# Two places for the exponentials of the first five units of an attention and FFN kernel

## The chip, the cores and the metric

The kernel runs on one core of a Trainium2 chip. A core has a tensor engine (PE; its weight loads are listed apart, as PEld), a vector engine (DVE), a scalar engine (ACT), GpSimd (POOL) and a queue that issues DMAs (SP). PE reads SBUF and writes PSUM; ACT and DVE read and write both. Each engine works through its own queue of instructions in order and waits where an instruction needs the result, or the buffer, of another engine. The metric is the device time of one execution in microseconds (us).

## The reference

Sparse attention for 8 batches of 8 heads, 576 positions and a head size of 64, and on its output an FFN with softplus:

```python
scores = scale * np.matmul(q, k.transpose(0, 1, 3, 2))
thresh = np.max(scores, axis=-1, keepdims=True) - tau
scores = np.where(scores >= thresh, scores, -1000000000.0)
scores = scores - np.max(scores, axis=-1, keepdims=True)
attn = np.exp(scores)
attn = attn / (np.sum(attn, axis=-1, keepdims=True) + 1e-09)
attn_out = np.matmul(attn, v)
x = attn_out.transpose(0, 2, 1, 3).reshape(B * S, H * D)
h = x @ w_in
g = np.maximum(h, 0.0) + np.log1p(np.exp(-np.abs(h)))
out = g @ w_out
```

x has 4608 rows of 512 columns, and the FFN is 2048 wide. Everything is float32.

## The kernel before, in words

**Units and tiles.** Two heads of a batch make a unit; there are 32. A unit's 2 x 576 query rows are 9 tiles of 128: tiles 0 to 3 belong to the first head, 5 to 8 to the second, and tile 4 (`NC`) holds the last 64 rows of both. `mate` (L451) names pairs: (0,1), (2,3), (5,6), (7,8); tile 4 is alone. 288 tiles run one after the other.

**What a tile passes through.** `scores` (L406) multiplies queries and keys into one of two PSUM banks, which tiles take by turns. `row_max` (L427) takes the negated row maximum and the threshold on DVE (L430, L431). `exps` (L434) writes exp(score - maximum), 128 x 576, into one half of `e_all` on ACT (L435). `mask` (L438) sets to zero on DVE, in place, what lies below the threshold, and adds up the rows (L440). `weights_T` (L458) transposes the 576 columns on PE, since the value product needs them in partitions: four transposes of 128 columns (L474), and the remaining 64 columns. `weights_hi` (L493) copies the transposed values to SBUF on ACT (L498, L510 to L514), `values` (L542) multiplies them with v.

**The halves of `e_all`.** `e_all` is 128 x 2 x 576. A tile in half 0 has its 512 main columns first and its 64 remaining ones last; a tile in half 1 has them the other way round (the keys are laid out as 64, 512, 64 columns, and `scores` starts at column 64 or at column 0). So the remaining columns of both halves lie side by side, and one transpose (L471), issued with the second tile of a pair, takes the 128 columns of both. The lone tile transposes its own 64 (L477). Before the change halves alternate from tile to tile over the whole kernel; since a unit has nine tiles, a pair's first tile is in half 0 in even units and in half 1 in odd ones.

**Whole units.** The first `NF = 5` units are "whole" (`s.whole`): their weights and values stay in float32, and the value products (L549) are float32 matmuls. Later units split weights into upper and lower parts (`group`, L444, tags `gH` and `gL` with two buffers each), which DVE computes (L132, a helper's line), and multiply both (L555, L556). So no buffer of the tag `gL` is used before unit 5.

**The order of the work.** A loop over the tiles (L924) goes through a string of steps, for tile g: `PAT0` for the first 36 tiles (`TG`), `PAT` after that.

```python
PAT = "ThRlefmpfxSvwp"
PAT0 = "RMTeShlfpfxvwp"
```

R is the row maximum of tile g+1, M the mask of tile g (m: of tile g+1), T its transposes, e the exponentials of tile g+1, S the scores of tile g+2, h and l the upper and lower parts of tile g, v three float32 value products, f FFN matmuls, x the next unit's splits and transposes, w and p the preparation of weights and steps put off. In the first 36 tiles transposes go to PSUM banks of their own (`tm`, `tr`), after that into the bank of the tile's scores (`s`).

From these calls the framework lays out each engine's queue: a step that comes first in the source has precedence, but one that is ready earlier by the framework's own estimate can go ahead. It also adds the waits, from the tiles and columns that instructions read and write.

**The preparation of weights** shares the queues in the first 60 or so tiles: for each of 32 pieces a load (SP, L185), then L193 on ACT, L194 on POOL, L200, L202 and L205 on DVE, and a split on POOL (lines 125 and 132 of helpers). Pieces of `w_in` are written back to DRAM (L234).

**The FFN** works in chunks of 512 rows: `hidden` (L632; matmuls L645, L647, L649), softplus on ACT (L667), `project` (L694; L703, L705, L707). Its matmuls begin with tile 41, are spread over the tiles, and fill the end alone.

Of the kernel before, what the change touches and what calls it, by code (L numbers as in the profile page):

```python
# [9 lines left out]
F32 = mybir.dt.float32  # L10
F32R = mybir.dt.float32r
# [12 lines left out]
P = 128  # L24
# [35 lines left out]
def tile_kernel(ctx: ExitStack, tc: tile.TileContext, q, k, v, tau, w_in, w_out, out):  # L60
# [8 lines left out]
    nc = tc.nc  # L69
    B, H, S, D = q.shape  # L70
    NT, DM = out.shape
    DFF = w_in.shape[1]
    SM = 512
    SR = S - SM
    HS = S // 2
    NC = SM // P
# [8 lines left out]
    apool = ctx.enter_context(tc.tile_pool(name="apool", bufs=2))  # L85
# [11 lines left out]
    ident = identr.bitcast(F32)  # L97
# [177 lines left out]
    for b in range(B):  # L275
        for kind in (("one", "two") if b < NSPLIT else ("all",)):
            for hp in range(NPAIR):
                s = Unit()
# [5 lines left out]
                for g, (j, members) in enumerate(groups):  # L284
                    c = 0
# [113 lines left out]

    e_all = cpool.tile([P, 2, S], F32, name="e_all")
    banks = [ps_s.tile([P, 2, 512], F32, tag="s", name=f"s_{i}") for i in range(SB)]
    nth = [0]

    def scores(s, t):  # L406
        if t == s.tiles[0]:
            s.sums = apool.tile([P, 9], F32, tag="sums", name=f"sums_{s.i}")
            s.half, s.sp, s.m, s.grp = {}, {}, {}, {}
        sp = banks[nth[0] % SB]  # L410
        s.half[t] = half = nth[0] % 2
        nth[0] += 1
        s.sp[t] = sp
        if t == NC:
            parts = [(qm[:, n, j, :], j) for j in range(2) for n in range(2)]
        else:
            j = 0 if t < NC else 1
            c = t if t < NC else t - NC - 1
            parts = [(s.qT[j][n][:, c * P:(c + 1) * P], j) for n in range(2)]
        k0 = (1 - half) * SR  # L420
        for m, (lhs, j) in enumerate(parts):
            for hf in range(2):
                i = nc.tensor.matmul(sp[:, hf, 0:HS], lhs, s.kT[j][:, k0 + hf * HS:k0 + (hf + 1) * HS],  # L423
                                     start=(m == 0), stop=(m == len(parts) - 1))
        scored.append(i)
# [6 lines left out]
        s.m[t] = (negm, thr)  # L432

    def exps(s, t):  # L434
        nc.scalar.activation(e_all[:, s.half[t], :].rearrange("p (h n) -> p h n", h=2), s.sp[t][:, :, 0:HS],  # L435
                             AF.Exp, bias=s.m[t][0], scale=1.0)

    def mask(s, t):  # L438
        e2 = e_all[:, s.half[t], :].rearrange("p (h n) -> p h n", h=2)
        masked.append(nc.vector.scalar_tensor_tensor(  # L440
            out=e2, in0=s.sp[t][:, :, 0:HS], scalar=s.m.pop(t)[1], in1=e2, op0=ALU.is_ge, op1=ALU.mult,
            accum_out=s.sums[:, s.tiles.index(t):s.tiles.index(t) + 1]))
# [8 lines left out]
    def mate(s, t):  # L451

        if t == NC:
            return None, False
        u = t if t < NC else t - 1
        return (t + 1, False) if u % 2 == 0 else (t - 1, True)

    def weights_T(s, t):  # L458
        half = s.half[t]
        e = e_all[:, half, :]  # L460
        other, second = mate(s, t)
        lone = other is None
        if 9 * NPAIR * s.b + 9 * s.hp + t < TG:
            main = ps_g.tile([P, NC, P], F32, tag="g", name=f"tm_{s.i}_{t}")
            rest = ps_g.tile([P, NC, P], F32, tag="g", name=f"tr_{s.i}_{t}")[:, 0, :] if lone or second else None
        else:
            sp = s.sp[t]
            main = sp[:, 0, :].rearrange("p (c n) -> p c n", n=P)
            rest = sp[:, 1, 0:P]
        if second:  # L470
            nc.tensor.transpose(rest, e_all.rearrange("p h n -> p (h n)")[:, SM:SM + P], ident)  # L471
        for c in range(NC):
            c0 = half * SR + c * P
            nc.tensor.matmul(main[:, c, :], e[:, c0:c0 + P], ident, is_transpose=True, start=True, stop=True)  # L474
        if lone:
            r0 = 0 if half else SM
            nc.tensor.transpose(rest[0:SR, :], e[:, r0:r0 + SR], ident)  # L477
        s.sp[t] = (main, rest)
# [358 lines left out]
    for kind, g in WL:  # L837
        for m in range(4):
            n = len(prep)
# [71 lines left out]
    for n in (0, 2, 1):  # L911
        qkT(u0, 1, n)
        point()
    u0.eng, u0.eng_lo = eng, nc.gpsimd
    scores(*tiles[0])
    row_max(*tiles[0])
    exps(*tiles[0])
    scores(*tiles[1])
    for j in range(2):
        split_v(u0, j)  # L920
# [3 lines left out]
    for g, (cur, t) in enumerate(tiles):  # L924
# [5 lines left out]
        for step in PAT0 + ("m" if g == TG - 1 else "") if g < TG else PAT:  # L930
            if step == "T":
                weights_T(cur, t)
            elif step == "h":
                weights_hi(cur, t)
            elif step == "l":
                weights_lo(cur, t)
            elif step == "R" and nxt:
                row_max(*nxt)
            elif step == "e" and nxt:
                exps(*nxt)  # L940
            elif step == "m" and nxt:
                mask(*nxt)
            elif step == "M":
                mask(cur, t)
            elif step == "f":
                upto += quota / PAT.count("f")
                while done < upto:
                    done += next(ffn)
            elif step == "x":
                extras(cur.i, cur.tiles.index(t))  # L950
            elif step == "S" and g + 2 < NS:
                scores(*tiles[g + 2])
            elif step == "v":
                slow_products()
            elif step == "w":
                while prep and prep[0][0] <= g:
                    _, f, a = prep.pop(0)
                    f(*a)
            elif step == "p":
                point()  # L960
# [38 lines left out]
```

## Time and profile before

| | |
|---|---|
| median of 3 runs | 1450.28 us (1449.85 to 1451.96) |
| the profiled execution | 1450.65 us, its span 1448.9 us |
| busy over the span | PE 97%, DVE 68%, ACT 59%, POOL 41% |
| mean of one exponential (L435) | 751 ns, x288 |
| mean of one mask (L440) | 815 ns, x288 |
| mean of one row maximum (L430) | 754 ns, x288 |
| mean of one transpose (L474) | 276 ns, x1008 |
| HBM traffic | 116 GB/s over the span |

PE's ends are modelled. "Idle before" (in rows of the timeline: the number in square brackets) is the time that the engine had nothing to do just before an instruction, with the instruction that ended it. In the timeline a row gives the start in us, the length in us, engine, line, operation, output and inputs, and the number of instructions merged into it. In the page's slices each digit is the busy share of a fortieth of the span (36 us) in tenths.

### The profile page before, as it was taken

The page shows a single profiled execution, that of the slowest core. Times are in us where ns is not written, and L with a number is a line of the kernel's source. Part 1 is how long each engine was busy: PE and PEld are TensorE (multiplying, and loading weights), DVE is VectorE, ACT ScalarE, POOL GpSimd, SP SyncE. Part 2 cuts the span into 40 slices and gives each one's busy share as a digit, 9 for nine tenths or more (in the row PEclk, how much of TensorE's full clock was granted, in tenths as well). Part 3 has the DMA queues.
Part 4 walks back from the last instruction along what each step waited for, and adds up shares of the span by engine and source line. Part 5 has one row for each costly group of instructions (what it writes and reads, how often), then busy time and mean ns, then how long its engine had stood idle before and what let it go on. Part 6 is the DMA issues. An engine that isn't in the chain of part 4 may idle for free.

```text
span 1448.9 us, 23497 instructions
## 1 busy us (share of the span) xinstructions
PE 1399.3 (97%) x7860; PEld 1161.6 (80%) x7860; DVE 983.1 (68%) x2211; ACT 848.1 (59%) x1615; POOL 591.0 (41%) x619
## 2 busy tenths in 40 slices
PE   6987999999999999999999999999999999999998
PEld 4654788878888888888888888888888888788886
DVE  6977688877777777777777777777777777402111
ACT  5766767767656566657665665667665765311010
POOL 3667666544333333344334333444334431324221
PEclk9999999999999999999999999999999999999999
DMA  5767765445333533444433533354344532344321
GB/s 160 220 192 231 212 187 170 138 121 154 109 102 110 137 115 110 119 134 150 123 111 96 153 106 101 116 151 120 113 119 136 148 98 74 101 130 129 119 85 44
DMA packets 131208, 189.93 MB, mean 131 GB/s; under 512 B 35312, under 2 KB 86800, under 8 KB 131088
## 3 DMA queue, kind: packets, MB, share of 16 engines
q1 hardware_dynamic: 131088, 188.43, 44.5%
q8 instruction: 63, 1.03, 0.3%
q14 instruction: 57, 0.47, 0.1%
HBM read 140.51 MB, written 27.41 MB: 116 GB/s over the span
## 4 chain that ended last, share of the span: by engine, by line
PE 78%; DVE 7%; ACT 5%; issue 3%; DMA 3%; POOL 2%; SPq 1%; POOLq 0%; ACTq 0%; DVEq 0%
PE s L423 10%; PE h L647 9%; PE h L645 9%; PE h L649 8%; PE o L707 8%; PE o L705 7%; PE s L474 7%; PE o L703 7%; PE pv L555 3%; PE pv L556 3%; PE tr L364 2%; DVE e_all L440 2%; DVE negm L430 2%; PE pv L549 1%; POOL g L132 1%
## 5 line engine op out<-in xcount | busy, mean ns | idle before, releaser
L132 POOL TENSOR_TENSOR g<-st,g 128x512 fp32r<-128x512 f32 x144 | 191.7, 1349 | 196.3 <-DVE g L129 182.5
L440 DVE SCALAR_TENSOR_TENSOR e_all<-s,thr,e_all 128x576 f32<-128x576 f32 x288 | 234.4, 815 | 53.0 <-ACT e_all L435 49.8
L430 DVE TENSOR_REDUCE negm<-s 128x1 f32<-128x576 f32 x288 | 217.1, 754 | 43.1 <-PE s L423 34.6
L435 ACT ACTIVATE e_all<-s,negm 128x576 f32<-128x576 f32 x288 | 215.9, 751 | 39.3 <-PE tr L471 20.7
L707 PE MATMUL o<-wo_o,g 128*128 128x512 f32 x576 | 232.3, 404 | 5.3 <-POOL g L132 5.3
L703 PE MATMUL o<-wo_o,g 128*128 128x512 f32 x576 | 232.0, 403 | 1.1 <-ACT st L667 0.7
L647 PE MATMUL h<-xl,wi 128*128 128x512 f32 x576 | 232.8, 404 | 0.0
L645 PE MATMUL h<-xh,wi 128*128 128x512 f32 x576 | 229.8, 399 | 0.0
L649 PE MATMUL h<-xh,wi 128*128 128x512 f32 x576 | 229.3, 398 | 0.0
L705 PE MATMUL o<-wo_o,g 128*128 128x512 f32 x576 | 228.5, 397 | 0.0
L498 ACT CAST gH<-s 128x512 fp32r<-128x512 f32 (+1 forms) x270 | 145.0, 550 | 139.1 <-PE s L474 135.6
L132 DVE TENSOR_TENSOR gL<-s,gH 128x512 fp32r<-128x512 f32 (+1 forms) x270 | 168.8, 634 | 47.8 <-ACT gH L498 25.3
L423 PE MATMUL s<-kT,qT 128*128 128x288 f32 x1024 | 192.2, 310 | 6.2 <-ACT gH L498 1.8
L423 PEld LDWEIGHTS s<-kT,qT 128*128 128x128 f32 x1024 | 148.5, 190 | 27.9 <-issue 11.3
L474 PE MATMUL s<-identr,e_all 128*128 128x128 f32 x1008 | 155.1, 276 | 4.8 <-DVE e_all L440 4.8
L129 DVE CAST g<-st 128x512 fp32r<-128x512 f32 x128 | 57.4, 485 | 149.5 <-ACT st L667 149.0
L667 ACT ACTIVATE st<-h 128x512 f32<-128x512 f32 x144 | 78.3, 596 | 115.3 <-PE h L649 114.6
L474 PEld LDWEIGHTS s<-identr,e_all 128*128 128x128 f32 x1008 | 114.7, 141 | 22.3 <-DVE e_all L440 12.6
L707 PEld LDWEIGHTS o<-wo_o,g 128*128 128x128 f32 x576 | 108.4, 188 | 29.1 <-POOL g L132 11.0
L645 PEld LDWEIGHTS h<-xh,wi 128*128 128x128 f32 x576 | 108.3, 188 | 23.5 <-issue 1.0
L703 PEld LDWEIGHTS o<-wo_o,g 128*128 128x128 f32 x576 | 108.5, 188 | 22.2 <-DVE g L129 2.0
L649 PEld LDWEIGHTS h<-xh,wi 128*128 128x128 f32 x576 | 108.4, 188 | 21.6
(107 smaller groups left out, 2366.4 us busy)
## 6 DMA issues: line engine op xcount, KB each, us to landing
wi<-wi_d SPq DMA_DIRECT2D x144, 512.0 KB
qT<-qT SPq DMA_DIRECT2D x124, 128.0 KB
R<-r_d SPq DMA_DIRECT2D x64, 144.0 KB
kn<-in_k_dram SPq DMA_DIRECT2D x32, 256.0 KB
qn<-in_q_dram SPq DMA_DIRECT2D x32, 256.0 KB
vn<-in_v_dram SPq DMA_DIRECT2D x32, 256.0 KB
wc_i<-in_moe_w_in_dram SPq DMA_DIRECT2D x16, 512.0 KB
wi_d<-wc_i SPq DMA_DIRECT2D x32, 256.0 KB
```

What stands on the lines that cost most here:

```text
L132: eng.tensor_tensor(out=out_, in0=in_, in1=hi.bitcast(F32), op=ALU.subtract)
L423: i = nc.tensor.matmul(sp[:, hf, 0:HS], lhs, s.kT[j][:, k0 + hf * HS:k0 + (hf + 1) * HS], start=(m == 0), stop=(m == len(parts) - 1))
L430: nc.vector.reduce_max(negm, s.sp[t][:, :, 0:HS], axis=AX.XY, negate=True)
L435: nc.scalar.activation(e_all[:, s.half[t], :].rearrange("p (h n) -> p h n", h=2), s.sp[t][:, :, 0:HS], AF.Exp, bias=s.m[t][0], scale=1.0)
L440: masked.append(nc.vector.scalar_tensor_tensor(out=e2, in0=s.sp[t][:, :, 0:HS], scalar=s.m.pop(t)[1], in1=e2, op0=ALU.is_ge, op1=ALU.mult, ...
L474: nc.tensor.matmul(main[:, c, :], e[:, c0:c0 + P], ident, is_transpose=True, start=True, stop=True)
L645: nc.tensor.matmul(h, wi[:, 0, cc, :], u.h[cc], start=(cc == 0), stop=False)
L647: nc.tensor.matmul(h, wi[:, 0, cc, :], u.l[cc], start=False, stop=False)
L649: nc.tensor.matmul(h, wi[:, 1, cc, :], u.h[cc], start=False, stop=(cc == NCC - 1))
L703: nc.tensor.matmul(o, gh[:, sl], wo[fc][:, 0, :], start=(i == 0), stop=False)
L705: nc.tensor.matmul(o, gh[:, sl], wo[fc][:, 1, :], start=False, stop=False)
L707: nc.tensor.matmul(o, gl[:, sl], wo[fc][:, 0, :], start=False, stop=(i == QF - 1))
```

## The change

In the whole units the exponentials of pairs go by turns to a second place, `e_more`, and to `e_all`; the lone tile counts as a pair here. `e_more` takes one of the two buffers of the tag `gL`. Which half a tile uses now follows from its place in the pair: the first and the lone tile take half 0, the second half 1, in all 32 units. The PSUM banks go on alternating as before. Units 5 to 31 use `e_all` alone, as before, with the new numbering of halves.

```diff
     e_all = cpool.tile([P, 2, S], F32, name="e_all")
+    e_more = apool.tile([P, NC, 320], F32R, tag="gL", name="e_more").bitcast(F32)
+    e_more = e_more.rearrange("p c n -> p (c n)")[:, 0:2 * S].rearrange("p (h n) -> p h n", h=2)
+    pairs = [0]
...
         sp = banks[nth[0] % SB]
-        s.half[t] = half = nth[0] % 2
+        half = s.half[t] = int(mate(s, t)[1])
+        pairs[0] += not half
+        s.e[t] = e_more if s.whole and pairs[0] % 2 else e_all
         nth[0] += 1
...
     def exps(s, t):
-        nc.scalar.activation(e_all[:, s.half[t], :].rearrange("p (h n) -> p h n", h=2), s.sp[t][:, :, 0:HS],
+        nc.scalar.activation(s.e[t][:, s.half[t], :].rearrange("p (h n) -> p h n", h=2), s.sp[t][:, :, 0:HS],
                              AF.Exp, bias=s.m[t][0], scale=1.0)
```

`mask` and both transposes of `weights_T` (L471, L474) read and write `s.e[t]` in place of `e_all` in the same way.

More of the change, by code (lines that the diff above doesn't have):

```diff
@@ L408, in scores @@
             s.sums = apool.tile([P, 9], F32, tag="sums", name=f"sums_{s.i}")
-            s.half, s.sp, s.m, s.grp = {}, {}, {}, {}
+            s.half, s.sp, s.m, s.grp, s.e = {}, {}, {}, {}, {}
         sp = banks[nth[0] % SB]
-        s.half[t] = half = nth[0] % 2
+        half = s.half[t] = int(mate(s, t)[1])
+        pairs[0] += not half
+        s.e[t] = e_more if s.whole and pairs[0] % 2 else e_all
         nth[0] += 1
@@ L434, in exps @@
     def exps(s, t):
-        nc.scalar.activation(e_all[:, s.half[t], :].rearrange("p (h n) -> p h n", h=2), s.sp[t][:, :, 0:HS],
+        nc.scalar.activation(s.e[t][:, s.half[t], :].rearrange("p (h n) -> p h n", h=2), s.sp[t][:, :, 0:HS],
                              AF.Exp, bias=s.m[t][0], scale=1.0)
     def mask(s, t):
-        e2 = e_all[:, s.half[t], :].rearrange("p (h n) -> p h n", h=2)
+        e2 = s.e[t][:, s.half[t], :].rearrange("p (h n) -> p h n", h=2)
         masked.append(nc.vector.scalar_tensor_tensor(
@@ L459, in weights_T @@
         half = s.half[t]
-        e = e_all[:, half, :]
+        e = s.e[t][:, half, :]
         other, second = mate(s, t)
@@ L470, in weights_T @@
         if second:
-            nc.tensor.transpose(rest, e_all.rearrange("p h n -> p (h n)")[:, SM:SM + P], ident)
+            nc.tensor.transpose(rest, s.e[t].rearrange("p h n -> p (h n)")[:, SM:SM + P], ident)
         for c in range(NC):
```

## The prediction

> **What bounds the kernel now.** I read the page's busy table and its slices first, then the windows of four stretches: busy time and, in brackets, instructions of PE, PE's weight loads, DVE, ACT and POOL, then PE's granted clock, the DMA share and GB/s.
>
> ```profile
> PE 1399.3 (97%) x7860; PEld 1161.6 (80%) x7860; DVE 983.1 (68%) x2211; ACT 848.1 (59%) x1615; POOL 591.0 (41%) x619
> ...
> PE   6987999999999999999999999999999999999998
> ```
>
> ```profile
> 20.00:146.00 126.00, 106.69 (x591) 71.74 (x590) 101.82 (x215) 85.16 (x195) 83.50 (x98) 0.95 0.71 204
> 52.30:69.30 17.00, 14.44 (x90) 10.34 (x91) 16.90 (x35) 12.07 (x30) 11.57 (x14) 1.00 0.66 185
> 86.80:109.60 22.80, 21.14 (x109) 13.15 (x109) 17.50 (x40) 13.71 (x30) 16.08 (x18) 0.93 0.64 171
> 200.00:1240.00 1040.00, 1027.38 (x6067) 878.88 (x6066) 794.02 (x1819) 679.29 (x1264) 411.32 (x429) 1.00 0.42 123
> ```
>
> From 200 us on, PE has 12.6 us without work in 1040, so nothing there pays that doesn't shorten PE's own work. In the first four slices there is slack: between 20 and 146 us (the attention tiles that run before the first FFN product) PE stands still for 126.0 - 106.7 = 19.3 us and DVE for 24.2. What the change frees lies there. Who waits for whom between 18 and 150 us (us in total, times, longest):
>
> ```profile
> ACT e_all L435 <- PE tr L471: 20.7, 12, 3.0
> ...
> DVE e_all L440 <- ACT e_all L435: 14.3, 17, 2.9
> ACT wa_i L193 <- DMA wc_i<-in_moe_w_in_dram: 11.0, 6, 4.1
> ...
> DVE wa_o L200 <- POOL wa_o L194: 6.1, 7, 1.3
> ```
>
> The first line is what the change is about. An exponential (L435) writes a half of `e_all`; the transpose L471 reads 64 columns of each half. So the exponential of a pair's first tile, and of the lone tile, waits until the previous pair's second tile has been masked on DVE and transposed on PE. The second line is how much DVE feels of this, at most. The other two are waits that the change leaves: the weight preparation, whose steps stand in the same queues of ACT, POOL and DVE.
>
> **Part 1: the wait that goes.** The longest wait of a mask in units 0 to 3 shows what it is worth.
>
> ```profile
> 24.46 2.41 PE L549 MATMUL pv<-gH,vn 128*64 128x256 f32 x6
> 24.56 0.76 DVE L430 TENSOR_REDUCE negm<-s 128x1 f32<-128x576 f32 x1
> ...
> 27.16 0.74 ACT L435 ACTIVATE e_all<-s,negm 128x576 f32<-128x576 f32 x1 [2.57 <-PE tr L471]
> ...
> 27.94 0.82 DVE L440 SCALAR_TENSOR_TENSOR e_all<-s,thr,e_all 128x576 f32<-128x576 f32 x1 [2.37 <-ACT e_all L435]
> ...
> 31.45 0.63 PE L474 MATMUL tm<-identr,e_all 128*128 128x128 f32 x4 [0.35 <-DVE e_all L440]
> ...
> 34.55 0.30 PE L471 MATMUL tr<-identr,e_all 128*128 128x128 f32 x1 [0.20 <-DVE thr L431]
> ```
>
> The row maximum ends at 25.32, so with a place of its own the exponential could run at about 25.4 and the mask at 26.2, 1.7 us sooner. But L471 came late because PE itself was at value products until 26.87, and in the 8 us after it PE stood still only 0.35 and 0.20 us. So 2.37 us of DVE's wait are worth 0.55 us of time. The other masks that waited for an exponential held by L471, up to unit 3's end:
>
> ```profile
> 69.36 0.82 DVE L440 SCALAR_TENSOR_TENSOR e_all<-s,thr,e_all 128x576 f32<-128x576 f32 x1 [0.16 <-ACT e_all L435]
> ...
> 92.33 0.82 DVE L440 SCALAR_TENSOR_TENSOR e_all<-s,thr,e_all 128x576 f32<-128x576 f32 x1 [0.97 <-ACT e_all L435]
> ...
> 98.60 0.82 DVE L440 SCALAR_TENSOR_TENSOR e_all<-s,thr,e_all 128x576 f32<-128x576 f32 x1 [0.43 <-ACT e_all L435]
> ...
> 103.90 0.82 DVE L440 SCALAR_TENSOR_TENSOR e_all<-s,thr,e_all 128x576 f32<-128x576 f32 x1 [0.47 <-ACT e_all L435]
> ...
> 109.66 0.33 PE L471 MATMUL tr<-identr,e_all 128*128 128x128 f32 x1 [1.41 <-DVE e_all L440]
> ...
> 127.60 0.82 DVE L440 SCALAR_TENSOR_TENSOR e_all<-s,thr,e_all 128x576 f32<-128x576 f32 x1 [0.18 <-ACT e_all L435]
> ```
>
> Only where PE idles soon after does a wait count: 0.16, 0.47 (1.41 of idle PE follows at 109.66) and 0.18. The 0.97 and 0.43 fall in a stretch, 86.8 to 109.6, in which PE's idle time of 1.7 is little more than that 1.41. Term: 0.55 + 0.16 + 0.47 + 0.18 = 1.4 us. Bounds: 0, if the weight steps wait in the mask's place, and all six waits, 4.6 us.
>
> **Part 2: the order of the queues.** The instructions are laid into the queues anew, and an exponential that is ready sooner can stand further ahead. Two places show a price.
>
> ```profile
> 18.47 0.76 DVE L430 TENSOR_REDUCE negm<-s 128x1 f32<-128x576 f32 x1 [1.43 <-PE s L423]
> ...
> 20.45 0.78 ACT L435 ACTIVATE e_all<-s,negm 128x576 f32<-128x576 f32 x1
> ...
> 22.14 0.66 PE L474 MATMUL tm<-identr,e_all 128*128 128x128 f32 x4 [2.06 <-DVE e_all L440]
> ...
> 81.07 0.43 DVE L200 TENSOR_SCALAR wa_o<-wa_o 128x512 uint32<-128x512 uint32 x1 [1.34 <-POOL wa_o L194]
> ...
> 82.14 0.81 DVE L440 SCALAR_TENSOR_TENSOR e_all<-s,thr,e_all 128x576 f32<-128x576 f32 x1
> ...
> 83.11 0.63 PE L474 MATMUL tm<-identr,e_all 128*128 128x128 f32 x4 [0.72 <-DVE e_all L440]
> ```
>
> At the start, the exponential of 20.45 could follow its row maximum at 19.2: 1.25 of the 2.06 us in which PE idles. At 82.14 the mask stands behind a weight step that waited 1.34 us for POOL; a mask that is ready earlier would be put ahead, worth PE's 0.72. Term: 2.0 us; bounds -3 and 5. Below nothing, because an order can also turn out worse (half of L200's 6.1 us of waits, with masks behind them); 5 is a quarter of PE's 19.3.
>
> **Part 3: unit 4 and the buffer.** One more long wait of a mask lies at this stretch's end:
>
> ```profile
> 146.10 0.82 DVE L440 SCALAR_TENSOR_TENSOR e_all<-s,thr,e_all 128x576 f32<-128x576 f32 x1 [2.86 <-ACT e_all L435]
> 146.16 0.47 PE L645 MATMUL h<-xh,wi 128*128 128x512 f32 x1
> ```
>
> From here the FFN products fill PE, so I count 0; bounds 0 and 2.9. The new place is one of two buffers that lie idle until unit 5, whose second group takes it over two tiles after its last reader: 0.
>
> **Part 4: the new numbering of halves.** A pair's first tile and the lone tile 4 now both take half 0. In units 5 to 31, with `e_all` alone, tile 5's exponential therefore waits for tile 4's transposes (L474, L477), which it didn't before. Mostly it comes after them anyway, behind tile 4's copies on ACT. At six of the 27 lone tiles (the first and the last are shown) it doesn't:
>
> ```profile
> 352.41 0.76 ACT L435 ACTIVATE e_all<-s,negm 128x576 f32<-128x576 f32 x1
> ...
> 353.45 0.27 PE L477 MATMUL s<-identr,e_all 128*64 128x128 f32 x1
> ...
> 1147.97 0.76 ACT L435 ACTIVATE e_all<-s,negm 128x576 f32<-128x576 f32 x1
> ...
> 1149.02 0.27 PE L477 MATMUL s<-identr,e_all 128*64 128x128 f32 x1
> ```
>
> The exponential starts 1.05 us ahead of L477 and will start after its end, at least 1.05 + 0.27 = 1.3 us later. Queued behind it on ACT are the lone tile's copies, or they go first and it comes 2 us later; behind the mask on DVE stand that tile's lower parts, and PE's transposes of tile 5 wait for the mask. What hides this is the FFN products, which can be laid before them. How well, the waits between 200 and 1300 us tell:
>
> ```profile
> DVE e_all L440 <- ACT e_all L435: 31.8, 57, 1.4
> ...
> PE s L474 <- DVE e_all L440: 3.7, 11, 0.4
> ```
>
> Of 31.8 us in which masks waited for exponentials PE felt 3.7, or 12%. Six times 1.3 to 2.0 us is 8 to 12 us; 12% of 10 is 1.2 us. Bounds: 0 and, if the cover is gone, 12.
>
> **The sum.** 1.4 + 2.0 + 0 - 1.2 = 2.2 us gained. The profiled execution took 1450.65 us (span 1448.9, 1.75 around it), 0.4 above the median of 1450.28, so it becomes 1448.4 by its own clock and 1448.1 beside the median. This case's own range goes from 5 us gained to 1 lost. A measurement of this kernel can tell about 0.2%, 2.9 us, from no change, so most of this case counts as none.
>
> **Rivals.**
>
> 1. DVE, not PE, paces the first stage. From 52.3 to 69.3 us it is busy 16.9 of 17 us. If that holds for the stage, each wait of a mask on a held exponential is worth its whole length: 4.6 us for the six waits, 1.25 at the start, 1.34 at 81 us and 0.8 at other such weight steps, 8 us; less the 1.2 of part 4, 6.8 gained: 1443.5, between 1440 and 1446. Against it: DVE itself idles 24.2 us in the stage, 11.0 of ACT's waits hang on loads and 6.1 of DVE's on POOL. Chance 0.28. The Trainium skill ("Perfetto Trace Analysis", Identifying the Most-Contended Engine) speaks for this rival: it calls matmul busy time a poor measure of PE's headroom, asks for the weight-load share instead, and takes DVE's occupancy at its word. By that rule PE's 71.74 of 126 us (57%) leave room, and DVE at 81% is the limit.
>
> 2. Slower: tile 5's exponential (part 4) reaches PE. The wait is new and certain, and two engines stand behind it; in those six places the scheduler had brought tile 5 forward, so other products must now fill the gap. With the 3.4 of parts 1 and 2 against it, it decides once over 60% of the 10 us reach PE (6.3 lost against 3.4 gained makes 2.9, the limit); from 60% to all 12 us the time is 1453 to 1459. Against it: the 12%. Chance 0.20.
>
> 3. The freed exponential waits for something else, for L193 ahead of it on ACT (11.0 us on loads), or its mask for L200 (6.1 us). The masks move and PE's idle time stays: within 1 us of 1450.3. For it: those waits are untouched. Against it: the start, where neither stands between. Chance 0.14.
>
> **How the numbers follow.** My case 0.38 (a third of it beyond 2.9 us gained), rival 1 0.28, rival 3 0.14, rival 2 0.20. Faster by over 0.2%: 0.12 + 0.28 = 0.40. Within: 0.26 + 0.14 = 0.40. Slower: 0.20. My case's range is 1445 to 1451; the whole range goes down to 1441, into rival 1, and up into rival 2, to 1454.
>
> **What would show it.** In the changed profile the waits of L435 on L471 must be gone up to the first FFN product (20.7 us to under 2) and masks must wait less than 14.3; PE's idle time between 20 us and that product must fall by 3 to 4 us and the product start as much before 146.16. L200's waits and L193's on loads should stay, near 6 and 11. At lone tiles after unit 4 no exponential of tile 5 may start before L477 has ended, and PE's waits on masks from 200 us should stay under 6. If the first FFN product comes 6 us or more earlier, rival 1 is right; if it comes earlier and the end doesn't, part 4 is mis-sized; if masks wait less and PE idles as before, rival 3.

## The result and the profile after

The changed kernel takes 1459.55 us in the median of four runs (1457.47 to 1461.08), beside 1450.07 us for the kernel before (four runs, 1449.38 to 1451.96): a ratio of 1.0063, 95% interval [1.0047, 1.0078]. It is some 9 us slower, where 2.2 us of gain were forecast. The profiled execution took 1457.47 us; it is the fastest of the four, so the profile below accounts for some 7 of the 9 us.

From the page of the changed kernel: busy time by engine, and PE's busy share in the 40 slices.

```profile
PE 1400.6 (96%) x7860; PEld 1161.2 (80%) x7860; DVE 984.0 (68%) x2211; ACT 851.9 (59%) x1615; POOL 589.1 (40%) x619
...
PE   6878999999999999999999999999999999999998
```

The work is the same, 1400.6 us of PE after 1399.3; what was added in the profiled execution is for the most part time in which PE stands still. The windows of three stretches say where. First the row of the kernel before that the prediction didn't show, then the rows of the changed kernel (columns as there: busy time and instructions of PE, its weight loads, DVE, ACT, POOL; PE's granted clock, DMA share, GB/s).

```profile
146.00:200.00 54.00, 53.05 (x286) 39.72 (x285) 37.64 (x78) 43.20 (x85) 33.54 (x39) 1.00 0.71 214
```

```profile
20.00:146.00 126.00, 105.59 (x594) 71.94 (x592) 100.33 (x214) 85.81 (x193) 77.66 (x94) 0.96 0.66 192
146.00:200.00 54.00, 50.37 (x260) 36.69 (x260) 34.38 (x73) 40.74 (x81) 35.80 (x38) 1.00 0.77 231
200.00:1240.00 1040.00, 1025.80 (x6050) 875.53 (x6049) 794.09 (x1814) 680.77 (x1263) 410.76 (x432) 1.00 0.43 123
```

PE's idle time: 20.4 us in place of 19.3 up to 146 us, 3.6 in place of 1.0 from there to 200, 14.2 in place of 12.6 up to 1240. That is 5.4 of the 6.8 us by which the two profiled executions differ. So the loss has two parts: one in the first 200 us, where the second place works, and one in the 27 later units, where only the numbering of halves differs.

The waits between 18 and 150 us of the changed kernel (us in total, times, longest), those that answer to the rows of before. First a second row of the kernel before for L200, which the prediction left out:

```profile
DVE wa_i L200 <- POOL wa_i L194: 2.7, 3, 1.4
```

```profile
ACT wa_i L193 <- DMA wc_i<-in_moe_w_in_dram: 9.2, 7, 3.4
...
ACT e_all L441 <- DVE negm L436: 8.3, 8, 2.0
...
DVE e_more L446 <- ACT e_more L441: 7.6, 7, 2.3
ACT e_more L441 <- DVE negm L436: 6.8, 8, 1.8
...
DVE wa_i L200 <- POOL wa_i L194: 5.8, 3, 2.3
...
DVE wa_o L200 <- POOL wa_o L194: 5.5, 7, 3.2
...
DVE e_all L446 <- ACT e_all L441: 3.4, 6, 1.1
```

Exponentials (now L441) no longer wait for L477, the former L471: the 20.7 us are gone. In their place they wait 15.1 us for their own row maxima (L436). Masks (L446) wait 11.0 us for exponentials, where it was 14.3. The weight step L200 waits longer for POOL than before, 11.3 us in place of 8.8 (6.1 + 2.7), and its longest waits are 2.3 and 3.2 us, where they were 1.4 and 1.3. What that does, the timeline of the changed kernel shows near 100 us:

```profile
100.41 0.74 ACT L441 ACTIVATE e_all<-s,negm 128x576 f32<-128x576 f32 x1
...
101.69 0.43 DVE L200 TENSOR_SCALAR wa_i<-wa_i 128x512 uint32<-128x512 uint32 x1 [2.31 <-POOL wa_i L194]
...
102.03 0.75 DVE L436 TENSOR_REDUCE negm<-s 128x1 f32<-128x576 f32 x1
...
102.70 1.27 DVE L202 SCALAR_TENSOR_TENSOR wa_i<-wc_i,wa_i 128x512 uint32<-128x512 uint32 x1
...
103.89 0.20 DVE L437 TENSOR_SCALAR thr<-negm,ntau 128x1 f32<-128x1 f32 x1
104.01 0.80 DVE L446 SCALAR_TENSOR_TENSOR e_all<-s,thr,e_all 128x576 f32<-128x576 f32 x1
...
104.88 0.33 PE L477 MATMUL tr<-identr,e_all 128*128 128x128 f32 x1 [3.32 <-DVE e_all L446]
```

The exponential is done at 101.15, but its mask starts at 104.01. Ahead of it in DVE's queue stands L200, which waits 2.31 us for POOL, and behind that another row maximum, a second weight step and a threshold. PE idles 3.32 us for this one mask. Two masks followed across this place show what it costs (tiles counted from 0). The one above, at 104.01, is tile 28's. Below are tile 27's and then, from the kernel before, tile 28's; tile 27's of before starts at 98.60 and stands in the prediction.

```profile
96.57 0.81 DVE L446 SCALAR_TENSOR_TENSOR e_all<-s,thr,e_all 128x576 f32<-128x576 f32 x1
```

```profile
101.89 0.80 DVE L440 SCALAR_TENSOR_TENSOR e_all<-s,thr,e_all 128x576 f32<-128x576 f32 x1
```

Tile 27's mask comes 2.03 us sooner than before, tile 28's 2.12 us later. So just ahead of this place the changed kernel led, and the one place turns a lead of 2 us into a lag of 2. Two more places at which PE waits for a mask behind L200:

```profile
78.44 1.27 POOL L132 TENSOR_TENSOR wo_o<-wa_o,wo_o 128x512 fp32r<-128x512 f32 x1
78.50 1.48 DVE L200 TENSOR_SCALAR wa_o<-wa_o 128x512 uint32<-128x512 uint32 x1 [0.59 <-POOL wa_o L194]
...
82.17 0.85 PE L480 MATMUL tm<-identr,e_more 128*128 128x128 f32 x4 [2.19 <-DVE e_more L446]
...
87.42 1.48 DVE L200 TENSOR_SCALAR wa_o<-wa_o 128x512 uint32<-128x512 uint32 x1 [0.20 <-POOL wa_o L194]
...
90.51 0.30 PE L477 MATMUL tr<-identr,e_all 128*128 128x128 f32 x1 [2.33 <-DVE e_all L446]
```

Here L200 waits for POOL only 0.59 and 0.20 us. What holds the mask is L200 itself: it takes 1.48 us, where it took 0.43 at 101.69. The last section comes back to this. Between L200 and the mask stand a row maximum, a threshold and L202 at the first place, a threshold and L202 at the second.

After the attention tiles the first FFN products wait too, for transfers and for parts of x, which none of them did before:

```profile
147.26 0.50 PE L651 MATMUL h<-xh,wi 128*128 128x512 f32 x1 [1.41 <-DMA wi<-wi_d]
...
159.99 0.50 PE L651 MATMUL h<-xh,wi 128*128 128x512 f32 x1 [0.83 <-ACT xh L127]
...
161.34 0.50 PE L653 MATMUL h<-xl,wi 128*128 128x512 f32 x1 [0.62 <-POOL xl L132]
```

### The profile page after: what moved, and what is told of

Same layout as the page of the kernel before. It is cut to its first block, busy times and chain, and to the rows that moved or that the text cites. A ratio compares the mean times of both kernels' runs of the same rounds, so it can differ in the third digit from the quotient of the medians.

```text
span 1455.7 us, 23484 instructions
## 1 busy us (share of the span) xinstructions
PE 1400.6 (96%) x7860; PEld 1161.2 (80%) x7860; DVE 984.0 (68%) x2211; ACT 851.9 (59%) x1615; POOL 589.1 (40%) x619
## 4 chain that ended last, share of the span: by engine, by line
PE 75%; ACT 7%; DVE 6%; issue 4%; DMA 4%; POOL 3%; SPq 2%; POOLq 0%; ACTq 0%
PE s L429 10%; PE h L651 8%; PE h L653 8%; PE h L655 8%; PE o L713 7%; PE o L711 7%; PE s L480 7%; PE o L709 7%; PE pv L562 3%; PE pv L561 3%; ACT L673 2%; PE tr L364 2%; ACT st L673 2%; DVE negm L436 1%; ACT gH L504 1%
## 5 line engine op out<-in xcount | busy, mean ns | idle before, releaser
L436 DVE TENSOR_REDUCE negm<-s 128x1 f32<-128x576 f32 x288 | 217.4, 755 | 50.9 <-PE s L429 38.8
L446 DVE SCALAR_TENSOR_TENSOR e_all<-s,thr,e_all 128x576 f32<-128x576 f32 x265 | 215.8, 816 | 35.3 <-ACT e_all L441 32.1
L441 ACT ACTIVATE e_all<-s,negm 128x576 f32<-128x576 f32 x265 | 198.7, 750 | 23.8 <-DVE negm L436 16.7
L480 PE MATMUL s<-identr,e_all 128*128 128x128 f32 x988 | 150.0, 274 | 4.7 <-DVE e_all L446 4.7
L651 PEld LDWEIGHTS h<-xh,wi 128*128 128x128 f32 x576 | 108.3, 188 | 27.0 <-DMA wi<-wi_d 1.6
L653 PEld LDWEIGHTS h<-xl,wi 128*128 128x128 f32 x576 | 108.3, 188 | 22.3 <-POOL xl L132 1.1
```

Of the source, the lines that this page charges most:

```text
L436: nc.vector.reduce_max(negm, s.sp[t][:, :, 0:HS], axis=AX.XY, negate=True)
L441: nc.scalar.activation(s.e[t][:, s.half[t], :].rearrange("p (h n) -> p h n", h=2), s.sp[t][:, :, 0:HS], AF.Exp, bias=s.m[t][0], scale=1.0)
L446: masked.append(nc.vector.scalar_tensor_tensor(out=e2, in0=s.sp[t][:, :, 0:HS], scalar=s.m.pop(t)[1], in1=e2, op0=ALU.is_ge, op1=ALU.mult, ...
L651: nc.tensor.matmul(h, wi[:, 0, cc, :], u.h[cc], start=(cc == 0), stop=False)
L653: nc.tensor.matmul(h, wi[:, 0, cc, :], u.l[cc], start=False, stop=False)
```

## The experiments

Ratios are to the kernel before, run on the same chip (medians of 1450.4 to 1450.8 us), with 95% intervals.

**The parts apart (e1 to e4).** e1 takes the numbering of halves alone, from unit 5 on (a pair's first tile and the lone tile share a half as in the change, but it is the other one); e2 the second place alone. The new numbering within the whole units is in neither; the queues of the changed kernel and of e2 are in the same order up to 197 us.

```diff
 # e1, in the kernel before
-        s.half[t] = half = nth[0] % 2
+        half = s.half[t] = nth[0] % 2 if s.whole else int(not mate(s, t)[1])
 # e2, in the changed kernel
-        half = s.half[t] = int(mate(s, t)[1])
-        pairs[0] += not half
+        s.half[t] = half = nth[0] % 2
+        pairs[0] += not mate(s, t)[1]
```

> One place for all exponentials, as before; only in units 5 to 31 a pair's first tile and the lone tile share a half, so that tile 5's exponential waits for the lone tile's transposes. The first 45 tiles are as before. Theory (the loss has two sources: the order of the queues in the first 36 tiles, and this numbering later): 3 to 5 us slower, since in the changed kernel tile 5's mask came 2.6 us later at six lone tiles and left 0.4 to 1.2 us behind each time. Rival (the loss lies in the first stage alone and is only handed down): within 1 us of 1450.

> The second place for pairs in the whole units, with halves alternating from tile to tile as before. Theory: 3 to 6 us slower, all of it by tile 45; after that masks keep their distance to the kernel before. Rival (the numbering of halves is all of the loss): 2 to 4 us faster than before, first FFN product at 142 to 144 us.

e1: 1453.01 us, 1.0018 [1.0009, 1.0026]; e2: 1455.57 us, 1.0038 [1.0025, 1.0051]. Together 0.56%, against 0.63% [0.47, 0.78] of the whole change: the two parts account for it. By these ratios the new numbering costs 2.6 us and the second place, with the order that comes with it, 5.5.

e3 and e4 split e2 once more, into the wait that goes and the order that comes with it. Each queue gets its order written out, by edges that order instructions and make none wait: e3 has both places in the order of before, e4 one place in the order of e2.

```diff
+    for name, text in ORDER.items():
+        turn = [traced[name][k] for k in array.array("H", zlib.decompress(base64.b85decode(text)))]
+        for i0, i1 in zip(turn, turn[1:]):
+            tc.add_manual_dep(i1, i0.name, mybir.DependencyInfo(
+                mybir.DependencyClass.NoSync, mybir.DependencyReason.DATA), reason="order")
```

> The second place with halves as before, and every engine's queue held in exactly the order that the kernel before has, by ordering edges on the same engine that add no wait. So only the wait for the transpose is gone. Theory (the wait was worth little, the order is what costs): 1 to 2 us faster than before, 1448 to 1449. Rival 1 (DVE paces the stage): 4 us faster or more. Rival 2 (earlier exponentials themselves disturb other engines): slower than 1451.

> The kernel before, one place, halves as before and the wait kept, but every queue in the order of the run with the second place alone. So only the order is changed. Theory (the order costs): slower than that run, by the waits that come back, 4 to 9 us slower than before. Rival (the order is of no account and something in the second place itself costs): within 1 us of 1450.

e3: 1450.8 us, 1.0001 [0.9992, 1.001]. e4: 1457.41 us, 1.0045 [1.0033, 1.0057]. The wait alone is worth nothing that can be measured, where 1 to 2 us had been expected; the order alone costs 6.5 us by its ratio. So the loss of e2 comes from the order, not from the places.

The way in which the order costs isn't the same in both. In e4 L200 waits only 6.4 us for POOL, less than before, and the exponentials wait 21.3 us for the transpose again. In the profile of e4, its median execution, PE's busy time is 1402.0 us after 1399.3, so 2.7 us of its loss are the same matmuls taking longer. Each run lists its granted clock, too: 0.995 to 0.999 in 23 executions of the kernel before, 0.990 to 0.996 in the six of e2, 0.993 to 0.996 in the five of e4. e2's slowest execution, 1460.07 us, has the 0.990, its fastest, 1453.38, a 0.996. So a part of what the order costs may come as a lower clock beside the idle time. But the profiled execution of the kernel before has 0.994 at 1450.65 us, so the listed clock alone doesn't set the time, and no run takes the two apart.

**Which part of the order (e6, e7).** e6 has e2's order but for three masks, those of tiles 22, 24 and 28, which go ahead of the weight steps on DVE, and so also of what stands between those and the masks. One of the three in DVE's queue (the listing of the program, without numbers):

```diff
+SCALAR_TENSOR_TENSOR e_all,sums<-s,thr,e_all 128x576
 TENSOR_SCALAR wa_i<-wa_i 128x512
 TENSOR_REDUCE negm<-s 128x1
 SCALAR_TENSOR_TENSOR wa_i<-wc_i,wa_i 128x512
 TENSOR_SCALAR thr<-negm,ntau 128x1
-SCALAR_TENSOR_TENSOR e_all,sums<-s,thr,e_all 128x576
```

e7 is e2's kernel and lets the framework find an order of its own, in which L200 comes a step later:

```diff
-            later_(1, lambda: second(0))
+            later_(2, lambda: second(0))
```

> The second place with its own new order of the queues, but three masks (tiles 22, 24 and 28, counted from 0) moved on DVE's queue ahead of the weight steps L200 and L202 that stand before them; all else in place. Theory (the new order costs because these three masks stand behind steps that wait for POOL; PE stood still for 2.2, 2.7 and 3.3 us there): at least 3 of the 5 us come back, 1452 or less. Rival (the loss is spread over the whole order): 1454 or more.

> The second place alone, and the first DVE step of a weight piece (L200) is put off by one more point, so that POOL has ended its part when DVE comes to it. The queues are laid out by the framework. Theory (masks behind L200 are what the new order costs): L200's waits of 11.5 us fall under 4 and the time to 1449 to 1453. Rival (later weights hold up the first FFN products instead): 1455 or more, with PE waiting on loads of weights at the first product.

e6: 1451.69 us, 1.0007 [0.9994, 1.002]. Three moved masks bring back about 4.5 of e2's 5.5 us (2 to 7 by the two intervals). The windows of e6 agree: PE's idle time is 18.3 us up to 146 and 1.8 from there to 200, where e2 has 19.9 and 3.0 and the changed kernel 20.4 and 3.6.

```profile
20.00:146.00 126.00, 107.72 (x601) 72.46 (x600) 100.22 (x216) 88.16 (x198) 80.11 (x96) 0.95 0.68 198
146.00:200.00 54.00, 52.23 (x274) 38.33 (x273) 37.31 (x77) 41.05 (x81) 35.16 (x39) 1.00 0.76 224
```

e7 missed: 1462.3 us, 1.0078 [1.0066, 1.0091]. L200's waits did fall, from 11.5 us in e2 to 5.9 (18 to 150 us), and the time rose by 6 us: their total doesn't tell the time. In the same stretch the weight steps L200, L202 and L205 took DVE 51.0 us in e7, 42.5 in e2 and 43.6 before, for 55 or 56 of them. Nine of e7's first 19 L200 start beside a two-input step of POOL and run long, two of e2's first 20; the last section has more of this. And the stalls moved; in e7's timeline PE waits 1.55 and 3.06 us for masks at 139 and 146 us:

```profile
139.37 0.33 PE L477 MATMUL s<-identr,e_all 128*128 128x128 f32 x1 [1.55 <-DVE e_all L446]
...
146.43 0.66 PE L480 MATMUL s<-identr,e_more 128*128 128x128 f32 x4 [3.06 <-DVE e_more L446]
```

**Why the wait is worth nothing (e5, e9, e11, e12).** In e3 the wait is gone and no queue is laid anew, yet the time is that of before. In its profile the first FFN product starts at 140.79 us, 5.4 us before that of the kernel before. But PE then stands still (e3's timeline; lines are shifted, L139 and L663 are the cast of x and the first FFN product):

```profile
152.25 0.62 ACT L139 CAST xh<-xst 128x512 fp32r<-128x512 f32 x1 [3.72 <-DMA xst<-x_d]
...
152.92 0.74 PE L663 MATMUL h<-xh,wi 128*128 128x512 f32 x1 [2.04 <-ACT xh L139]
```

The last quarter of the FFN's first chunk comes from the pair of heads that unit 3 computes, and its load holds PE. So my next theory was that the freed time is taken back at this load. e5 loosens the load in e3, and e9 does the same with one place, in the kernel before; both read that quarter from another pair, so they leave a dependency out.

```diff
-            nc.sync.dma_start(st[:, c:c + m], x_d[b][:, cc, o:o + m])
+            src = cc - 1 if u.n == 0 and cc == NCC - 1 else cc
+            nc.sync.dma_start(st[:, c:c + m], x_d[b][:, src, o:o + m])
```

e11 and e12 keep the load and make it come sooner: unit 3's scaling of x goes ahead of two other steps in POOL's queue, e11 with two places, e12 with one.

```diff
 TENSOR_TENSOR xl<-xst,xh 128x512
+TENSOR_TENSOR xp<-xp,R 128x576
 TENSOR_TENSOR wo_o<-wa_o,wo_o 128x512
 TENSOR_TENSOR xl<-xst,xh 128x512
-TENSOR_TENSOR xp<-xp,R 128x576
```

> The second place with the old order of the queues, and the last quarter of the first FFN chunk's input is read from another head pair's output, its load standing ahead of that pair's stores in SP's queue; so this kernel leaves out that one dependency (its FFN gets the wrong columns there). Theory (what the removed wait gained in the first stage is handed back at this load, on which a cast on ACT waited 3.7 us and PE 2.0): 2 to 4 us faster than the kernel before, 1447 to 1449. Rival (the lead is worth nothing anyway, because PE has its other work): as with the old order alone, within 1 us of before.

> The kernel before, with its one place and its wait, all queues in the order of e5, and e5's loosened load: the last quarter of the FFN's first chunk is read from another pair of heads (it leaves out that one dependency, so the FFN multiplies other columns). It is e5 without the second place. Theory 1 (the second place frees time that the wait for x takes back): this kernel keeps the time of before, ratio 0.9995 to 1.0005, and e5's 1.75 us need the second place. Theory 2 (e5's gain came from the loosened load alone, and the wait removed by the second place is worth nothing at all): ratio near e5's, 0.998 to 0.999, 1447.5 to 1449 us.

> e3 (two places, every queue in the order of before) with one instruction moved: on POOL unit 3's scaling of x goes ahead of two steps (a split of w_out and a lower part of x), so that it can run near 140.8 us instead of 143.7 and the load of the last quarter of the FFN's first chunk comes near 145 us instead of 148.1. Theory 1 (the time that the second place frees is taken back at that load): PE's wait of 2.04 us on the cast of x near 152.9 us goes or falls under 0.5, ratio 0.9985 to 0.9993. Theory 2 (the wait that the second place removes is worth nothing): 1.000 as in e3, with the wait gone or not.

> The kernel before, one place, queues in its own order, with e11's single move on POOL: the control for e11. There PE does not wait on the load of x, so theory 1 expects no change, 0.9995 to 1.0005, and e11 faster than this one by 0.7 us or more. Theory 2 (the move is worth something by itself, or nothing is worth anything): the same ratio as e11 within 0.0007.

| | one place | two places |
|---|---|---|
| order of before | 1 | e3 1.0001 [0.9992, 1.001] |
| load of x loosened | e9 0.9989 [0.998, 0.9998] | e5 0.9988 [0.9978, 0.9997] |
| scaling of x sooner | e12 0.999 [0.9981, 0.9999] | e11 0.9988 [0.9978, 0.9998] |

The theory falls. A sooner load is worth about 0.1%, 1.5 to 1.7 us by the ratios, but to the kernel with one place as well. With the load out of the way the second place changes the ratio by 0.0001 and 0.0002, each known to about 0.0013. So no gain from the wait on L471 shows, load or no load. What the sooner load is worth to the kernel with one place isn't settled: in e12's profile PE idles no less than before, and its busy time is 3.1 us shorter (1396.2 after 1399.3). And of e3's 5.4 us only 0.9 were idle time; the windows up to the first FFN product of before, e3 and e12:

```profile
20.00:146.16 126.16, 106.85 (x592) 71.90 (x592) 101.89 (x216) 85.32 (x196) 83.66 (x98) 0.95 0.71 204
```

```profile
20.00:140.79 120.79, 102.37 (x593) 69.39 (x592) 101.87 (x216) 85.83 (x195) 80.09 (x95) 0.99 0.73 212
```

```profile
20.00:143.42 123.42, 103.94 (x591) 70.31 (x592) 101.75 (x215) 84.70 (x194) 79.45 (x95) 0.97 0.72 206
```

PE's idle time is 19.3, 18.4 and 19.5 us. The other 4.5 us of e3's lead are the same matmuls at a granted clock of 0.99 in place of 0.95, and e12 with its one place gets 2.9 us of that kind. An early FFN product in a single profile is no evidence here.

Where the freed time goes can be read at one of the places that the prediction counted, 0.47 us at 103.90. The timeline of before, and below it that of e11, whose L212 is L200 and whose L489 is L471:

```profile
106.41 0.61 POOL L194 TENSOR_SCALAR wa_i<-wa_i 128x512 f32<-128x512 f32 x1
...
107.05 0.43 DVE L200 TENSOR_SCALAR wa_i<-wa_i 128x512 uint32<-128x512 uint32 x1 [1.42 <-POOL wa_i L194]
```

```profile
106.33 0.43 DVE L212 TENSOR_SCALAR wa_i<-wa_i 128x512 uint32<-128x512 uint32 x1 [1.97 <-POOL wa_i L206]
...
108.94 0.33 PE L489 MATMUL tr<-identr,e_more 128*128 128x128 f32 x1 [1.44 <-DVE e_more L458]
```

The mask no longer waits 0.47 us; the weight step behind it waits 0.55 us longer for POOL; and PE idles 1.44 us at the transpose after that, where it idled 1.41 (the row at 109.66 in the prediction).

**Whether the weight steps are the pace (e8, e13).** If L200's wait were all, masks put ahead of it would let the gain through. e8 moves eight masks of units 2 and 3 so, in e3's order; e13 adds e11's sooner scaling, so that the load of x is out of the way as well.

> The second place with the old order of the queues, and eight masks of units 2 and 3 (tiles 20, 22, 23, 25, 27, 30, 31, 33) moved on DVE's queue ahead of the weight step L200 that stood before them. Theory (in the old order too masks behind L200 hold PE, 1.9, 1.4, 1.2 and 1.3 us at the longest, but the lead is handed back at the first chunk's input): PE's idle time before the first FFN product falls by 3 us or more, the time only to 1449 to 1450.5. Rival (the lead stays): 1447 or less.

> e8 (two places, order of before, the masks of eight tiles of units 2 and 3 ahead of the weight step L200) together with e11's move on POOL, so that the load of x no longer holds what is gained. It tells apart why the second place is worth nothing even where that load is out of the way (e11 against e12). Theory 1 (in the order of before the time that a mask gains is spent in L200's wait for POOL, which stands ahead of a later mask): with those masks ahead of L200 the gain comes through, 1 us or more below e11, ratio 0.998 or less. Theory 2 (the chain through POOL and the loads of the weights sets the pace wherever the masks stand): the ratio of e11, 0.9983 to 0.9993.

e8: 1450.62 us, 1.0001 [0.9991, 1.001]; e13: 1448.89 us, 0.9992 [0.9983, 1.0001]. No gain over e3 and e11. Up to the first FFN product PE idles 18.4 us in e8, where a fall by 3 us or more had been expected, and 16.9 in e13, 2.4 less than before, though e13 is no faster than e12 with its 19.5. So a microsecond or two of idle time in one profile doesn't show in the time either. In e13 the wait of L200 near 104 us is down to 0.31 us, and the next one in the chain shows in the timeline:

```profile
107.06 0.66 ACT L205 ACTIVATE wa_i<-wc_i 128x512 f32<-128x512 f32 x1 [3.77 <-DMA wc_i<-in_moe_w_in_dram]
107.63 0.72 ACT L453 ACTIVATE e_all<-s,negm 128x576 f32<-128x576 f32 x1
...
109.36 0.63 PE L492 MATMUL tm<-identr,e_all 128*128 128x128 f32 x4 [2.26 <-ACT gH L530]
```

L205 here is L193 of before. It waits 3.77 us for a piece of `w_in`; the exponential and copies stand behind it on ACT, and with the last of these copies (L530) the 2.26 us end in which PE idles. At this place the preparation of weights, through DVE or through ACT, sets the pace. That it does so at every place of the stage isn't shown.

## Why the prediction was wrong

**Part 2, the order of the queues, is the step that failed.** It was put at 2.0 us gained, between 3 lost and 5 gained. Measured, the order costs 5.5 us with the second place and 6.5 without it, outside the bound. The place named for that bound was the right one, masks behind L200: moving three of them ahead brought back most of it (e6). But the size was taken from L200's waits in the old order, half of 6.1 us; that is one of two rows, and both make 8.8. The cost isn't the sum of these waits. At 104 us one wait of 2.31 us, a row maximum, a second weight step and a threshold add up ahead of one mask, and PE idles 3.32 us. At the other two places L200 hardly waits and takes 1.48 us itself. And in e4 and e7 L200's waits are below those of before, while they lose 6.5 and 11 us.

The gain was drawn from two favourable places, which assumes that the new queue is the old one with masks moved ahead. It was another queue. At the start nothing came of the 1.25 us. The exponential ends at 20.88 there, but a row maximum that waits for its scores stands between it and its mask, and the transposes start at 22.16, where they started at 22.14:

```profile
20.61 0.76 DVE L436 TENSOR_REDUCE negm<-s 128x1 f32<-128x576 f32 x1 [1.02 <-PE s L429]
...
22.16 0.66 PE L480 MATMUL tm<-identr,e_all 128*128 128x128 f32 x4 [1.58 <-DVE e_all L446]
```

At 82 us the mask does come sooner, at 81.30 in place of 82.14, but PE is ready 2.4 us sooner than before, and waits 2.19 us for it, where it waited 0.72.

**Part 1, the wait that goes**, 1.4 us gained between 0 and 4.6. The waits went as forecast, but no gain is left: e3 lies between 1.2 us gained and 1.4 lost, and e5 beside e9 and e11 beside e12 agree. That is the lower bound with the reason given for it, that the weight steps wait in the mask's place; the rows show this at the place near 104 us, and at the others it is argued. In the profile of e3 0.9 us of PE's idle time go, nearly half a microsecond of it at the start: 2.06 us of idle PE before the first transposes became 1.58.

**Part 3** stood: no cost of the buffer showed in e3, as far as its 1.4 us tell.

**Part 4, the numbering of halves**, 1.2 us lost between 0 and 12: right in sign, and mis-sized, 2.6 us [1.3, 3.8] in e1. The mechanism can be read at the last of the six lone tiles in the changed kernel: tile 5's exponential, which started 1.05 us ahead of the lone tile's transpose, now follows it.

```profile
1155.42 0.27 PE L483 MATMUL s<-identr,e_all 128*64 128x128 f32 x1
...
1156.47 0.75 ACT L441 ACTIVATE e_all<-s,negm 128x576 f32<-128x576 f32 x1
...
1157.77 0.82 DVE L446 SCALAR_TENSOR_TENSOR e_all<-s,thr,e_all 128x576 f32<-128x576 f32 x1
```

PE's waits on masks after 200 us are 4.5 us after the change and 3.7 in e1, as before. So the 12% by which it was sized didn't see the cost. PE's idle time between 200 and 1240 us did rise, from 12.6 to 14.2 and, in e1, to 14.1. In e1 it rose before the score products (L423), which wait for the lower parts on DVE, and not before the transposes; busy time, mean, and behind the second bar the idle time ahead of them, from 200 us on, before and in e1:

```profile
L423 PE MATMUL s<-kT,qT 128*128 128x288 f32 x840 | 154.5, 306 | 3.2 <-DVE gL L132 1.5 <-DVE gH L132 0.4
```

```profile
L423 PE MATMUL s<-kT,qT 128*128 128x288 f32 x840 | 155.3, 307 | 4.9 <-DVE gL L132 1.6 <-DVE gH L132 1.0
```

Many of the pieces are too short for the rows to name what ended them. In the changed kernel the same listing has 4.3 us before the score products and 4.5 before the transposes. In e1, too, the queues of the later units are laid anew, and no run holds their order; so the new wait and the new order aren't told apart here.

**The rivals.** Rival 1 has DVE as the pace. The Trainium skill ("Perfetto Trace Analysis", Identifying the Most-Contended Engine) speaks for it: it takes DVE's occupancy at its word. The runs don't agree: e3 takes some 6 us of the masks' waits for exponentials away and gains nothing, 1.0001 [0.9992, 1.001], and in the changed kernel those waits fall by 3.3 us while the time rises. Of the idle time that DVE has, 8.8 us are L200 at the head of its queue waiting for POOL. Rival 2 ended on the right side, with under a third of the loss. Rival 3 named the place, the mask behind L200 and the exponential behind L193, and held it for neutral: with the old order it is (e3, e13), with the new one most of the loss lies there (e6).

**The signs.** L441's waits on L477 went, as said; the masks' waits fell; both are true of a slower kernel. The sign on L200's waits, "near 6 and 11", failed with 11.3 us in all in place of 8.8, but it isn't a sign of the time: e4 and e7 have 6.4 and 5.9 and lose 6.5 and 11 us all the same. The sign that told was PE's idle time up to the first FFN product: it rose to 21.7 us (127.26 - 105.59) where a fall of 3 to 4 was forecast:

```profile
20.00:147.26 127.26, 105.59 (x595) 71.95 (x593) 100.61 (x215) 87.07 (x196) 78.92 (x95) 0.96 0.67 193
```

## What to carry to other kernels

Before crediting a removed wait, follow the freed instruction one step further in its queue: where the next instruction waits for another engine or a load, the time only changes its name. A removed dependency also lays in-order queues anew, and that can cost more than the wait was worth, where an instruction that another engine needs ends up behind steps that wait or run long; pin the old order once and try the wait and the order apart. The version to build on here is e12: one place, with one step moved ahead on POOL so that a load comes sooner, 0.999 [0.9981, 0.9999]; e11, with two places, is no faster.

## What the hardware showed that was not expected

The granted clock in the first stage differs between executions whose PE queue is the same: 0.95 in before, 0.97 in e12, 0.99 in e3, which moves the first FFN product by up to 4.5 us of PE's busy time, with idle times within 1.1 us of each other. One profile of this stage can't tell effects of a few microseconds.

The same weight step takes 0.43 us or 1.47 us on DVE. The timeline of e13, where POOL has nothing to do at the first and runs two-input steps beside the second:

```profile
79.09 0.43 DVE L212 TENSOR_SCALAR wa_o<-wa_o 128x512 uint32<-128x512 uint32 x1 [0.29 <-POOL wa_o L206]
...
82.66 1.41 POOL L611 TENSOR_TENSOR xp<-xp,R 128x576 f32<-128x576 f32 x1
...
82.89 1.47 DVE L212 TENSOR_SCALAR wa_o<-wa_o 128x512 uint32<-128x512 uint32 x1
...
84.03 1.45 POOL L144 TENSOR_TENSOR wo_o<-wa_o,wo_o 128x512 fp32r<-128x512 f32 x1
```

The second L212 starts 0.23 us after POOL's step and ends at 84.36, 0.29 us after that step's end: it took 1.04 us longer than the first, as if it had waited for most of it. It isn't a single case. Of the 99 steps of L200 in the first 156 us of five profiles (before, the changed kernel, e2, e7, e13), the 21 that start while POOL runs a two-input step take 0.73 to 1.64 us, and every one ends 0.28 or 0.29 us after POOL's step. None that starts with POOL idle takes over 0.45. The Trainium skill ("SBUF — State Buffer", Who interferes with whom) has a rule for this: such an operation can take the pair of ports that DVE shares with GpSimd, and whichever of the two issues second waits for the other to end. The rows agree with it, but for the 0.14 us by which such a step ends sooner than 0.43 us after POOL's. Masks stand behind such steps in DVE's queue: in the changed kernel this is what makes L200 take 1.48 us at 78.50 and 87.42, ahead of two of the three masks that e6 moved. In number these long steps don't explain the loss, since the kernel before has three of them, as the changed one has; what differs is where they stand.
